# Attention and a gated FFN on one core: weights' parts kept in the buffers from pass to pass, the pairs of chunks taken in the opposite order, and the second pass's sums tied on VectorE

## The chip, the core and the metric

The kernel runs on one core of a Trainium2 chip. Its engines are TensorE (PE: matmuls, and PEld: its weight loads), VectorE (DVE), ScalarE (ACT), GpSimd (POOL) and SyncE (SP), which here issues the DMAs. Each engine takes its instructions in order and waits for the others by semaphores. The metric is the device time of one launch in microseconds (us); less is better.

## The reference

```python
# 8 batches, 8 heads, 576 tokens, head size 64; keys and values averaged over 8 tokens
k_p, v_p = k.reshape(B, H, 72, 8, D).mean(3), v.reshape(B, H, 72, 8, D).mean(3)
attn = softmax(q @ k_p.T / sqrt(D))            # 1e-9 added to the sum
x = (attn @ v_p) -> (B * S, H * D)              # 4608 x 512
out = (sigmoid(x @ w_gate) * (x @ w_val)) @ w_out   # 512 -> 1536 -> 512
```

All is f32. The weights come as 64-bit floats and are converted on the core.

## The kernel before

**Number format.** Each f32 operand is split into a high and a low half that TensorE multiplies at its faster f32 rate (`split`: the high half is a cast on ACT, L103, the low half a subtract on DVE, L104). A product of two operands is three matmuls: high by high, high by low, low by high.

**Passes.** The 4608 tokens are 12 blocks of 384 (`BT`), two blocks (side 0 and side 1) in a pass, six passes, n = 0 to 5. Each pass has a hidden stage (gate G and value V, 12 chunks `f` of 128 hidden columns, or `NP` = 6 pairs `p` of chunks), then the second product with w_out. The attention of the next blocks runs in between: `next(tasks)` lets one piece of it into the program.

- Pass 0 is plain: `hidden_first` converts w_gate and w_val pair by pair, keeps the halves in DRAM (`kept`, and the words themselves in `kept_w`) and multiplies with `whole` (L582). `second` converts w_out chunk by chunk (`convert_o`: the load of `raw_o` L251, the conversion L122 to L132 on ACT and DVE, its halves `oparts`, the stores to `keptO` L258 and `keptwO` L260) and accumulates over all chunks (L717) with `hs`, the halves of the hidden values (L709, L710).
- Passes 1 to 5 take a pair of chunks and the two sides together as 2 by 2 blocks and multiply them with seven products in place of eight (`product`, L542: m = 1 to 7, in the order of `SLOTS`). For that sums of the weights' blocks are needed (`add_up` and `sums`, on DVE) and sums of the operand x (`sums_of_x`, `operands`; their halves are `xo1` to `xo7`, m by m, and plain chunks use `xo1`, `xo2` for side 0 and `xo5`, `xo4` for side 1). `second_sums` does the same for w_out (L808), with reloaded `oparts` (L279, L281) and `hs` of sums (`operand`, L771, L772).
- Pass 1 is mixed: `hidden_second` takes the last two pairs (f = 8 to 11) plain, while the sums for the first four pairs are made, then calls `hidden` for those four.

**Buffers.** `wpool`, "parts", has 8 buffers, just one pair's groups: G and V, each A to D (A, B, C hold two products' parts, 512 KB; D one, 256 KB, in passes 1 to 5). When the last product of a group is issued, `loaded` reloads its buffer for the next pair (L242), and at the end of a pass for pair 0. `big` has 4 buffers that hold `raw_o`, `hs`, the copies `o` of the results, the words `w8` of the weights being summed, and `s1`; `opool` has 4.

**What sets the order.** Nearly everything is put in order by a scheduler that simulates the program as written; it deals the instructions onto the engines, and the buffers of a pool onto its tiles. Only instructions given to `keep_in_program_order` (through `pinned`, or `in_turn` where `tied[0]` is set) stay in the order of the code among themselves. In the kernel before, `tied[0]` is never set. SP issues the loads and the stores in one queue, so an issue that waits holds back the ones behind it.

## Time and profile before

| | |
|---|---|
| runs shown | 998.54, 996.95 and 1000.31 us, median 998.54 |
| profiled execution | 994.61 us, its span 992.8 |
| granted clock of TensorE | 0.991 over the span |
| 0 to 176 us | first blocks' attention, pass 0 hidden |
| 176 to 241.4 us | pass 0, `second` |
| 241.6 to 276 us | pass 1, plain chunks (f = 8 to 11) |
| then to 350, and 350 to 408 us | pass 1: seven products, second product |
| 408, 550, 712 and 868 us | starts of the hidden stages of passes 2, 3, 4 and 5; their second products start at 500, 655, 808 and 950 |

How to read it: the stages are found in the timeline of TensorE, by its lines (L717, L582, L542, L808). The number that counts is TensorE's idle time in a stage and what ended it. A row of waits reads: engine, line that waited, what it waited for, us in total, times, the longest. A row of a timeline reads: start, duration, engine, line, operation, out<-in, count, and in brackets the idle time before and its releaser; "SPq" is SP's queue, where each row is the issuing of DMAs.

### The profile page before, as it was taken

What the parts mean: (1) busy time and instruction counts of PE and PEld (TensorE: products, weight loads), DVE (VectorE), ACT (ScalarE), POOL (GpSimd) and SP (SyncE); (2) the same over time, 40 slices, a digit from 0 to 9 for tenths busy, and PEclk for the clock granted to TensorE, in tenths of its full rate; (3) what the DMA queues carried; (4) which work ended last, traced back from release to release, by engine and by line L of the source; (5) the groups of instructions that cost most, each with busy time, mean ns of one, the idle gap of its engine ahead of it and who ended that gap; (6) DMA issues with size and microseconds to landing.
All of it is one profiled execution on the core that took longest, in us unless ns stands there. A gap on an engine that the chain in (4) does not pass through costs nothing.

```text
span 992.8 us, 15583 instructions
## 1 busy us (share of the span) xinstructions
PE 952.2 (96%) x5436; PEld 914.6 (92%) x5436; DVE 711.3 (72%) x1240; ACT 547.0 (55%) x1113; POOL 49.0 (5%) x67
## 2 busy tenths in 40 slices
PE   5779999989999999999999999999999999999998
PEld 4669999768999999998999999999999999999998
DVE  5767898688798889685588657679366669244474
ACT  4647677545376766564565556556365546233342
POOL 2010000000000100000000000000000100000000
PEclk9989999999999999999999999999999999999999
DMA  9736999876999978899778877787876677877567
GB/s 333 252 118 211 337 367 371 281 262 239 349 332 359 305 239 274 305 391 365 246 254 251 276 240 253 264 283 244 294 260 213 220 256 252 290 229 250 180 198 226
DMA packets 121773, 269.72 MB, mean 272 GB/s; under 512 B 12640, under 2 KB 50272, under 8 KB 120160
## 3 DMA queue, kind: packets, MB, share of 16 engines
q1 hardware_dynamic: 121696, 268.74, 80.2%
q8 instruction: 43, 0.70, 0.3%
q14 instruction: 34, 0.28, 0.1%
HBM read 212.06 MB, written 56.62 MB: 271 GB/s over the span
## 4 chain that ended last, share of the span: by engine, by line
PE 81%; DMA 8%; DVE 7%; ACT 3%; issue 1%; SPq 0%; ACTq 0%; DVEq 0%
PE chain L542 36%; PE acc L808 19%; PE chain L582 12%; PE acc L717 4%; PE sc L368 3%; PE av L377 3%; DMA oparts<-keptS 1%; PE tp L456 1%; PE vp L1011 1%; DVE s L741 1%; DVE hs L772 1%; DMA parts<-keptG1D 1%; DMA keptS<-sums 1%; DMA oparts<-keptO 1%; DMA w<-keptwO 1%
## 5 line engine op out<-in xcount | busy, mean ns | idle before, releaser
L542 PE MATMUL chain<-xo,parts 128*128 128x384 f32 x2352 | 438.3, 340 | 4.1 <-ACT sV L548 2.4
L542 PEld LDWEIGHTS chain<-xo,parts 128*128 128x128 f32 x2352 | 407.6, 188 | 8.2 <-ACT sV L548 3.2
L808 PE MATMUL acc<-hs,oparts 128*128 128x384 f32 x1260 | 229.5, 336 | 5.0 <-DMA oparts<-keptS 2.3
L808 PEld LDWEIGHTS acc<-hs,oparts 128*128 128x128 f32 x1260 | 218.2, 188 | 8.2 <-DVE hs L772 3.5
L582 PE MATMUL chain<-xo,parts 128*128 128x384 f32 x624 | 118.0, 343 | 3.2 <-ACT parts L170 3.1
L582 PEld LDWEIGHTS chain<-xo,parts 128*128 128x128 f32 x624 | 110.1, 191 | 4.9 <-ACT parts L170 3.7
L554 DVE TENSOR_TENSOR y<-chain,sG 128x384 f32<-128x384 f32 x84 | 46.1, 552 | 78.6 <-ACT sG L548 27.2
L554 DVE TENSOR_TENSOR y<-chain,sV 128x384 f32<-128x384 f32 x84 | 45.8, 549 | 43.0 <-PE chain L542 25.4
L450 POOL TENSOR_TENSOR pm<-e,rz 128x384 f32<-128x384 f32 x40 | 37.8, 945 | 682.3 <-DVE rz L431 365.2
L772 DVE TENSOR_TENSOR hs<-h,hs 128x768 fp32r<-128x768 f32 x60 | 57.4, 960 | 15.6 <-ACT hs L771 15.6
L560 ACT ACTIVATE gate<-y 128x384 f32<-128x384 f32 x84 | 43.8, 525 | 41.8 <-DVE y L554 41.4
L771 ACT CAST hs<-h 128x768 fp32r<-128x768 f32 x60 | 50.1, 835 | 30.2 <-PE acc L808 27.5
L548 ACT COPY sG<-chain 128x384 f32<-128x384 f32 x84 | 39.8, 476 | 48.3 <-PE chain L542 47.5
L548 ACT COPY sV<-chain 128x384 f32<-128x384 f32 x84 | 39.9, 476 | 43.1 <-PE chain L542 40.6
L717 PE MATMUL acc<-oparts,hs 128*128 128x512 f32 x216 | 55.1, 407 | 4.1 <-ACT hs L709 4.1
L717 PEld LDWEIGHTS acc<-oparts,hs 128*128 128x128 f32 x216 | 40.6, 193 | 14.1 <-ACT hs L709 5.3
L771 ACT CAST hs<-s 128x768 fp32r<-128x768 f32 x45 | 37.1, 835 | 25.3 <-PE acc L808 17.0
L563 DVE TENSOR_TENSOR h<-y,gate 128x384 f32<-128x384 f32 x84 | 47.5, 568 | 1.9
L772 DVE TENSOR_TENSOR hs<-s,hs 128x768 fp32r<-128x768 f32 x45 | 42.3, 951 | 5.6 <-ACT hs L771 5.3
L368 PE MATMUL sc<-kbd,raw 128*128 128x144 f32 (+1 forms) x256 | 43.2, 298 | 0.4 <-DVE y L554 0.4
L368 PEld LDWEIGHTS sc<-kbd,raw 128*128 128x128 f32 (+1 forms) x256 | 33.9, 177 | 7.9 <-issue 4.7
L460 DVE TENSOR_TENSOR pl<-tp,ph 128x384 fp32r<-128x384 f32 x40 | 22.0, 551 | 17.2 <-ACT ph L459 17.0
(168 smaller groups left out, 1183.5 us busy)
## 6 DMA issues: line engine op xcount, KB each, us to landing
oparts<-keptS SPq DMA_DIRECT2D x60, 512.0 KB, 4.9
oparts<-keptO SPq DMA_DIRECT2D x90, 256.0 KB, 3.8
raw<-in_wgv SPq DMA_DIRECT2D x12, 1024.0 KB, 7.5
raw<-in_qT SPq DMA_DIRECT2D x42, 192.0 KB, 4.7
raw<-in_kT SPq DMA_DIRECT2D x28, 288.0 KB, 5.2
out<-o SPq DMA_DIRECT2D x40, 192.0 KB, 4.7
raw<-in_vm SPq DMA_DIRECT2D x24, 256.0 KB, 4.6
raw_o<-in_wo SPq DMA_DIRECT2D x12, 512.0 KB, 5.9
```

The lines of the kernel that those rows point to most:

```text
L368: nc.tensor.matmul(sc[lo - i * P:hi - i * P, i], lhsT=q[:, lo:hi], rhs=kbd[slot(b, p)], start=True, stop=True)
L450: nc.gpsimd.tensor_tensor(out=pm, in0=e[:, n, :, :KM], in1=rz[:, n, :, None].broadcast_to([P, 2 * QT, KM]), op=ALU.mult)
L542: nc.tensor.matmul(t, lhsT=w[:, h, a], rhs=x[:, y, c], start=(m in (1, 2, 5) and c == 0 and k == 0), stop=(c == 1 and k == 2), skip_group_ ...
L548: nc.scalar.copy(s, t)
L554: nc.vector.tensor_tensor(out=y, in0=t, in1=seen[kind, {2: 1, 3: 6, 7: 5}[m]], op=ALU.add)
L560: nc.scalar.activation(gates[q[0]][:, q[1]], y, AF.Sigmoid)
L563: nc.vector.tensor_tensor(out=hb[f // 4][:, f % 4, q[0] * BT:(q[0] + 1) * BT], in0=y, in1=gates[q[0]][:, q[1]], op=ALU.mult)
L582: nc.tensor.matmul(t, lhsT=w[:, c // 2, h, a], rhs=x[:, y, c % 2], start=(c == 0 and k == 0), stop=(c == NC - 1 and k == 2),)
L717: nc.tensor.matmul(acc[i], lhsT=hs[:, y, a], rhs=o[:, w], start=(f == 0 and k == 0), stop=(f == NF - 1 and k == 2),)
L771: nc.scalar.copy(hs[:, 0], x)
L772: nc.vector.tensor_tensor(out=hs[:, 1], in0=x, in1=hs[:, 0].bitcast(F32), op=ALU.subtract)
L808: nc.tensor.matmul(acc[name, c], lhsT=w[:, k, h, c * P:(c + 1) * P], rhs=hs[:, y, k], start=(m in (1, 2, 5) and i % 3 == 0 and k == 0 and ...
```

## The change

1. `TURNS` gives the order of pairs in each pass: 0 to 3 in pass 1, then 3, 2, 1, 0, 4, 5, then 5 down to 0, 0 up to 5, 5 down to 0. The last pair of a pass is the first of the next, so its parts stay in the buffers (`stays`), and `loaded` no longer reloads at the end of a pass.
2. `reload_plain` goes: the plain chunks f = 8 to 11, made in pass 0, stay in their buffers until pass 1 (`gated` keeps them), and no longer come back from DRAM. Pair 0's parts are now reloaded two groups at a time between those chunks, and the last at their end.
3. In `hidden_second`, `tied[0]` is set around `prepare` and `sums`, so that their first subtracts and the splits of `sums` keep the code's order on ACT and DVE.
4. The thirds of w_out (`qs`) follow the order of the pairs.

```diff
     def sums(kind, p):
...
-        nc.vector.tensor_tensor(out=s[:, 0:2], in0=w[:, 1:3], in1=w[:, 0:2], op=ALU.subtract)
+        in_turn(nc.vector.tensor_tensor(out=s[:, 0:2], in0=w[:, 1:3], in1=w[:, 0:2], op=ALU.subtract))
...
-    def product(kind, p, m):
+    def product(kind, p, m, stays=False):
-        t, w, x = bank[kind, b], parts.pop((kind, p, m)), xo[m]
+        t, w, x = bank[kind, b], parts[kind, p, m] if stays else parts.pop((kind, p, m)), xo[m]
...
     def gated(f, side):
-        if side:
+        if side and f < 2 * EARLY:
             del plain["G", f], plain["V", f]
...
     def hidden_first(tasks):
-        for kind in "GV":
-            for f in range(2):
-                reload_plain(kind, 2 * EARLY + f)
...
+    TURNS = {1: (0, 1, 2, 3), 2: (3, 2, 1, 0, 4, 5), 3: (5, 4, 3, 2, 1, 0), 4: (0, 1, 2, 3, 4, 5), 5: (5, 4, 3, 2, 1, 0)}
...
     def hidden_second(tasks):
+        ring = [("G", "A"), ("G", "B"), ("G", "C"), ("V", "A"), ("G", "D"), ("V", "B"), ("V", "C"), ("V", "D")]
         for i, f in enumerate(range(2 * EARLY, NF)):
-            if f + 2 < NF:
-                for kind in "GV":
-                    reload_plain(kind, f + 2)
             if i < 3:
+                tied[0] = True
                 prepare("GV"[i % 2], i // 2)
+                tied[0] = False
             if i in (2,3,):
+                tied[0] = True
                 sums("O", made_o.pop(0))
+                tied[0] = False
...
+            if i:
+                for _ in range(2):
+                    reload(ring[0][0], 0, ring.pop(0)[1], True)
...
     def hidden(last, tasks, n):
-        pairs = EARLY if n == 1 else NP
-        for p in range(pairs):
+        pairs = TURNS[n]
+        for p, pair in enumerate(pairs):
...
-                product(kind, at, m)
-                loaded(kind, at, m, left, last, pairs, n == 1)
+                stays = at + 1 == len(pairs) and not last
+                product(kind, pairs[at], m, stays)
+                if at + 1 < len(pairs):
+                    loaded(kind, pairs[at], m, left, pairs[at + 1], n == 1)
...
     def second_sums(n, last, build, later):
-                    product("V", pairs - 1, 4)
-                    loaded("V", pairs - 1, 4, {}, last, pairs)
+                    product("V", TURNS[n][-1], 4, not last)
```

The lines of the new program stand 1 to 7 above or below those of the old one (L542 is L535, L582 is L575, L242 is L235, L251 is L244, L260 is L253). The engines' work is the same in number; on SP's queue 48 loads fewer stand. Up to the end of `hidden_first` TensorE's order is the same; behind it the scheduler deals nearly all anew. Three places:

**SP's queue at the end of pass n = 4.** Reloads of parts, and the first loads of w_out's sums (`keptS`) for `second_sums`. Before:

```order
L242 DMA parts<-keptG0C 128x1024
L242 DMA parts<-keptV0A 128x1024
L242 DMA parts<-keptG0D 128x512
L242 DMA parts<-keptV0B 128x1024
L242 DMA parts<-keptV0C 128x1024
L281 DMA oparts<-keptS_208 128x1024
L281 DMA oparts<-keptS_209 128x1024
L242 DMA parts<-keptV0D 128x512
L281 DMA oparts<-keptS_210 128x1024
L281 DMA oparts<-keptS_211 128x1024
L281 DMA oparts<-keptS_212 128x1024
```

After:

```order
L235 DMA parts<-keptV5A 128x1024
L235 DMA parts<-keptG5D 128x512
L235 DMA parts<-keptV5B 128x1024
L235 DMA parts<-keptV5C 128x1024
L235 DMA parts<-keptV5D 128x512
L274 DMA oparts<-keptS_208 128x1024
L274 DMA oparts<-keptS_209 128x1024
L274 DMA oparts<-keptS_210 128x1024
L274 DMA oparts<-keptS_211 128x1024
L274 DMA oparts<-keptS_212 128x1024
```

The reload of V0D, which waits for the last product of the pass, stood among the loads of `keptS`; now the pass's own last part, V5D, is loaded ahead of them, and nothing stands between.

**SP's queue in `second`, from about chunk f = 4 on.** `raw_o` with its buffer's number is one chunk of w_out: before, 2080, 2114, 2148 and 2182 are f = 4 to 7; after, 2068, 2102, 2136, 2170 and 2204 are f = 4 to 8. Before:

```order
L251 DMA raw_o_2148<-in_wo 128x1024
L260 DMA keptwO2_182<-raw_o_2080 128x256 x2
L298 DMA raw_2831<-in_vm 128x512
L258 DMA keptO4_196<-oparts_2087 128x1024
L294 DMA raw_2961<-in_qT 128x384
L251 DMA raw_o_2182<-in_wo 128x1024
L260 DMA keptwO2_182<-raw_o_2114 128x256 x2
L291 DMA raw_2964<-in_kT 128x576
L294 DMA raw_3010<-in_qT 128x384
L258 DMA keptO5_197<-oparts_2121 128x1024
```

After:

```order
L253 DMA keptwO2_182<-raw_o_2068 128x256 x2
L244 DMA raw_o_2102<-in_wo 128x1024
L291 DMA raw_2827<-in_vm 128x512
L251 DMA keptO4_196<-oparts_2075 128x1024
L244 DMA raw_o_2136<-in_wo 128x1024
L287 DMA raw_2937<-in_qT 128x384
L253 DMA keptwO2_182<-raw_o_2102 128x256 x2
L251 DMA keptO5_197<-oparts_2109 128x1024
L244 DMA raw_o_2170<-in_wo 128x1024
L253 DMA keptwO3_185<-raw_o_2136 128x256 x2
L251 DMA keptO6_198<-oparts_2143 128x1024
L244 DMA raw_o_2204<-in_wo 128x1024
```

Before, the load of f = 6 (2148) stands ahead of the store of f = 4's words (keptwO2, from 2080). After, it stands behind it, as those of f = 7 and 8 stand behind the stores of f = 5 and 6; and the load of f = 5 (2102) is behind the store of f = 4. In the new dealing the `raw_o` of f = 4, 6, 8 and 10 have one and the same of the four buffers, those of f = 5, 7, 9 and 11 another.

**DVE and TensorE where the plain chunks of pass 1 begin.** `xo4` is the operand for the second half of side 1, `s4` and `sums` are w_out's sums, `w8` the words of G and V being summed (2589 is G's pair 1, 2890 is V's pair 1). DVE before:

```order
L205 TENSOR_TENSOR s4_2610<-w4_2608 128x512
L415 TENSOR_REDUCE m_2974<-sc_2969 128x6
L206 TENSOR_TENSOR s4_2610<-w4_2608,s4_2610 128x256
L104 TENSOR_TENSOR sums_2614<-s4_2610,sums_2614 128x2x256
L207 TENSOR_TENSOR s4_2610<-w4_2608,s4_2610 128x256
L497 TENSOR_TENSOR s_2463<-xs1_1541 128x768
L694 COPY o_2406<-acc_2026 128x512
L104 TENSOR_TENSOR xo4_2361<-xs1_1541,xo4_2361 128x768
L497 TENSOR_TENSOR s_2464<-s_2463,xs0_966 128x768
L104 TENSOR_TENSOR sums_2619<-s4_2610,sums_2619 128x2x256
L694 COPY o_2413<-acc_2038 128x512
L104 TENSOR_TENSOR xo6_2536<-s_2464,xo6_2536 128x768
```

DVE after:

```order
L190 TENSOR_TENSOR w8_2589<-w8_2589 128x256
L205 TENSOR_TENSOR s4_2596<-w4_2594 128x512
L206 TENSOR_TENSOR s4_2596<-w4_2594,s4_2596 128x256
L207 TENSOR_TENSOR s4_2596<-w4_2594,s4_2596 128x256
L104 TENSOR_TENSOR sums_2600<-s4_2596,sums_2600 128x2x256
L188 TENSOR_TENSOR w8_2890<-w8_2890 128x512
L104 TENSOR_TENSOR sums_2605<-s4_2596,sums_2605 128x2x256
L189 TENSOR_TENSOR w8_2890<-w8_2890 128x256
L490 TENSOR_TENSOR s_2445<-xs1_1541 128x768
L190 TENSOR_TENSOR w8_2890<-w8_2890 128x256
L408 TENSOR_REDUCE m_2576<-sc_2571 128x6
L104 TENSOR_TENSOR xo4_2349<-xs1_1541,xo4_2349 128x768
```

TensorE before, from the last of `second` on (`xo1` and `xo2` are side 0's operands):

```order
L437 MATMUL tp_2697<-identr_89,r3_2693 96x128 x3
L582 MATMUL chain_2435<-xo1_2250,parts_1968 128x384 x6
L582 MATMUL chain_2435<-xo2_2287,parts_1968 128x384 x6
L582 MATMUL chain_2467<-xo5_2324,parts_1968 128x384
L582 MATMUL chain_2449<-xo1_2250,parts_1974 128x384 x6
L582 MATMUL chain_2449<-xo2_2287,parts_1974 128x384 x6
L582 MATMUL chain_2467<-xo5_2324,parts_1968 128x384 x5
L582 MATMUL chain_2467<-xo4_2361,parts_1968 128x384 x6
L582 MATMUL chain_2481<-xo5_2324,parts_1974 128x384 x6
L582 MATMUL chain_2481<-xo4_2361,parts_1974 128x384 x6
```

TensorE after, some 70 matmuls into the plain chunks:

```order
L575 MATMUL chain_2548<-xo5_2312,parts_x_1307 128x384 x3
L370 MATMUL av_1846<-ph_1832,vh1_97 128x384
L370 MATMUL av_1846<-pl_1833,vh1_97 128x384
L370 MATMUL av_1846<-ph_1832,vl1_102 128x384
L370 MATMUL av_1846<-pr_1760,vres1_107 128x384
L575 MATMUL chain_2548<-xo5_2312,parts_x_1307 128x384 x3
L361 MATMUL sc_2571<-kbd4_95,raw_2563 128x144
L361 MATMUL sc_2571<-kbd4_95,raw_2563 64x144
L361 MATMUL sc_2571<-kbd3_94,raw_2563 64x144
L361 MATMUL sc_2571<-kbd3_94,raw_2563 128x144
L575 MATMUL chain_2449<-xo4_2349,parts_1238 128x384
L575 MATMUL chain_2463<-xo4_2349,parts_x_1302 128x384
```

The low half of `xo4` moved on DVE from right behind the first copy of `o` to behind the sums of V's pair 1; on TensorE its first use moved from behind 30 plain matmuls to behind 72, two value products of the attention and a group of scores.

More of the change, by code (lines that the diff above doesn't have):

```diff
@@ L682, in hidden, with loaded @@
             pass
-    def loaded(kind, p, m, left, last, pairs=NP, fresh=False):
+    def loaded(kind, p, m, left, then, fresh):
         g, i = place(m)
         left[kind, p, g] = left.get((kind, p, g), 0) + 1
-        if left[kind, p, g] == sum(m != 8 for m in GROUPS[g]) and not (last and p + 1 == NP):
-            reload(kind, (p + 1) % pairs, g, fresh and p + 1 < pairs)
+        if left[kind, p, g] == sum(m != 8 for m in GROUPS[g]):
+            reload(kind, then, g, fresh)
     def store(o, r, acc, eng):
@@ L755, in third_sums @@
         minus(quarter(q, 1, 0), quarter(q, 0, 0), quarter(q, 1, 0))
-    qs = [(2, 0, 1) if n == 1 else (0, 1, 2) for n in range(NB // 2)]
+    qs = {n: [p // 2 for p in t[::2]] for n, t in TURNS.items()}
+    qs[1] = [2] + qs[1]
     halves = {}
```

20 lines of the change are left out of this document (7 added, 13 removed).

## The prediction

> **What bounds the kernel now.** I read the page first: its busy times, the chain and the queue.
>
> ```profile
> span 992.8 us, 15583 instructions
> PE 952.2 (96%) x5436; PEld 914.6 (92%) x5436; DVE 711.3 (72%) x1240; ACT 547.0 (55%) x1113; POOL 49.0 (5%) x67
> PE 81%; DMA 8%; DVE 7%; ACT 3%; issue 1%; SPq 0%; ACTq 0%; DVEq 0%
> q1 hardware_dynamic: 121696, 268.74, 80.2%
> ```
>
> TensorE is the bound: busy for 96% of the span, and 81% of the chain. The transfers are many, but the chain spends 8% on them. So a change that only takes transfers away can win no more than what TensorE waits for. What it waits for stands in its waits, asked first for the first pass's second product (176 to 242 us), then for all behind it (four of nine rows):
>
> ```profile
> PE acc L717 <- ACT hs L709: 4.1, 3, 2.0
> ...
> PE chain L542 <- ACT sV L548: 2.4, 2, 1.5
> PE acc L808 <- DMA oparts<-keptS: 2.3, 2, 1.6
> PE acc L808 <- DVE hs L772: 2.3, 3, 1.0
> ...
> PE chain L542 <- DMA parts<-keptG1B: 0.4, 1, 0.4
> ```
>
> After 242 us no wait is dear, and reloaded parts are waited for once, for 0.4 us. The table by stage says where there is slack (span, PE, PEld, DVE, ACT, POOL busy, clock, DMA share, GB/s):
>
> ```profile
> 176.00:242.00 66.00, 61.88 (x284) 49.07 (x283) 51.71 (x95) 34.63 (x74) 3.80 (x4) 0.97 0.74 250
> 242.00:266.00 24.00, 24.00 (x139) 24.00 (x138) 22.09 (x41) 11.98 (x23) 0.00 (x0) 1.00 1.02 354
> 266.00:350.00 84.00, 82.02 (x495) 79.70 (x494) 71.75 (x153) 55.92 (x125) 6.87 (x6) 1.00 0.96 329
> ```
>
> From 242 to 266 us, where the second pass's plain chunks run, three resources are full at once: TensorE, DVE (22.09 of 24.00) and the transfers (share 1.02). A different order costs most there.
>
> **The removed transfers.** By the order, 32 reloads at four pass boundaries and 16 reloads of plain chunks go, about 19 of 269.7 MB. The wait above prices them: −0.4 us at most. They are hidden by TensorE's own work, which has the next pair's parts in time. Term −0.4, bounds −0.4 and 0. What goes with them is small: a pass's last pair stays in its eight buffers, its products read it a second time at the start of the next pass, and only then is the second pair of that pass loaded into them, group by group, as between any two pairs before. So the cover of those loads is one pair's products, as it was, and I see no new wait at a pass's start. The buffers of the plain chunks f=8 to 11 that now stay from pass 0 to pass 1 cost no instruction either; their place is the reloads'.
>
> The Trainium skill, "Perfetto Trace Analysis", section "Identifying the Most-Contended Engine", says to work on the engine that is used most, and to judge TensorE by its weight-load share: here 92%, so it is TensorE, as the chain says. By that rule alone 19 MB less on the queues would change nothing, and the sum would be 0.
>
> **The ends of the passes.** SP's queue and TensorE at the end of pass n=4:
>
> ```profile
> 812.04 1.50 SPq L281 DMA_DIRECT2D oparts<-keptS  x2
> 816.03 0.32 SPq L242 DMA_DIRECT2D parts<-keptV0D  x1
> 816.44 4.25 SPq L281 DMA_DIRECT2D oparts<-keptS  x3
> ...
> 815.84 4.85 PE L808 MATMUL acc<-hs,oparts 128*128 128x384 f32 x27
> 822.33 18.99 PE L808 MATMUL acc<-hs,oparts 128*128 128x384 f32 x108 [1.64 <-DMA oparts<-keptS]
> ```
>
> The reload of V0D waits for the last V4 product (the matmuls behind it start at 815.84), and three loads of w_out's sums wait behind it on the queue; TensorE runs dry for 1.64 us. In the new order V5D's load comes earlier, the wrapped reloads are gone, and S_208 to S_212 stand together. So the 1.64 goes. Next late is then an hs from DVE, as at the same point of pass n=3, where the wait is DVE's:
>
> ```profile
> 670.56 4.09 PE L808 MATMUL acc<-hs,oparts 128*128 128x384 f32 x22 [0.86 <-DVE hs L772]
> ```
>
> Of the 2.3 us for oparts the other 0.7 falls in another pass, behind loads that also shared the queue with wrapped reloads; I take half of it. Term −2.0; bounds −2.3 (all) and 0 (hs is as late).
>
> **The second product of pass 0.** No line of it is edited, but its instructions are dealt anew. Its loop of `raw_o` buffers:
>
> ```profile
> 209.87 5.99 PE L717 MATMUL acc<-oparts,hs 128*128 128x512 f32 x18 [1.96 <-ACT hs L709]
> ...
> SPq L251 <- PE acc L717: 7.4, 5, 2.7
> ...
> 178.34 0.52 SPq L251 DMA_DIRECT2D raw_o<-in_wo  x1
> 191.59 0.86 SPq L260 DMA_DIRECT2D keptwO<-raw_o  x2
> 215.89 0.33 SPq L251 DMA_DIRECT2D raw_o<-in_wo  x1
> 225.14 0.84 SPq L260 DMA_DIRECT2D keptwO<-raw_o  x2
> ...
> keptwO<-raw_o SPq DMA_DIRECT2D x24, 128.0 KB, 4.2
> ```
>
> Before, a raw_o load waits for the matmuls of four chunks ago (5 times, 7.4 us on the queue). In the new order the `raw_o` of even and odd chunks share one buffer each, so from f=6 on each load stands right behind the keptwO store of the chunk two before, and must wait until that has landed. A turn is then load to store plus landing: 13.3 us for f=4 (178.34 to 191.59) and 9.3 for f=10 (215.89 to 225.14), plus 4.2. I take 14, nearest to f=10, when DVE had least other work (13.5; f=4 gives 17.5). The chains start earlier, since of 16 plain reloads only three loads, pair 0's first, are left in that part of the queue: I estimate f=4's parts ready at 182 (its load at about 171, not 178.34) and f=5's at 192 (its load is behind f=4's store, some 10 us). Then f=10 is ready at 224, f=11 at 234, and the product, 18 matmuls long per chunk (4.3 us), ends at about 238.5, where before it ended at 241.4: −2.9. But the new order puts two value products and two groups of scores of block 3 behind the stage, which TensorE still has to do:
>
> ```profile
> 184.68 0.34 PE L377 MATMUL av<-ph,vh 128*128 128x384 f32 x1
> ...
> 185.38 1.25 PE L368 MATMUL sc<-kbd,raw 128*128 128x144 f32 x8
> 186.37 4.16 PE L717 MATMUL acc<-oparts,hs 128*128 128x512 f32 x17
> ```
>
> That is 0.7 (184.68 to 185.38) and 1.0 (to 186.37), twice: +3.4. Term +0.5. Bounds: −4.1, all three waits of before gone; and +6.5, with turns of 16 us, as f=11 comes three turns behind f=5, so 6 us later (T at 244.5).
>
> **The plain chunks of pass 1.** This term decides. Let T be the end of the product (241.4 before). xo4 holds half of side 1's tokens' operand. Before, DVE makes its low half at 241.89, right behind the first copy of o, and TensorE has it in time (it is full there). In the new order its low half stands behind `add_up` of V1 (w8_2890): the tied sums keep the program's order on DVE, and the scheduler puts V1's subtract ahead. Rows of before:
>
> ```profile
> 241.60 25.45 PE L582 MATMUL chain<-xo,parts 128*128 128x384 f32 x144
> ...
> 248.56 1.21 SPq L187 DMA_DIRECT2D w<-keptwG  x1
> 252.86 0.32 SPq L187 DMA_DIRECT2D w<-keptwV  x1
> ...
> w<-keptwV SPq DMA_DIRECT2D x6, 512.0 KB, 5.5
> ...
> 238.63 0.60 DVE L415 TENSOR_REDUCE m<-sc 128x6 f32<-128x432 f32 x1
> 240.42 0.95 DVE L497 TENSOR_TENSOR s<-xs 128x768 f32<-128x768 f32 x1
> 241.89 0.95 DVE L104 TENSOR_TENSOR xo<-xs,xo 128x768 fp32r<-128x768 f32 x1
> 258.88 0.68 DVE L188 TENSOR_TENSOR w<-w 128x512 f32<-128x512 f32 x1
> 260.29 0.41 DVE L189 TENSOR_TENSOR w<-w 128x256 f32<-128x256 f32 x1
> ```
>
> V1's words were loaded at T+11.4 (252.86): their buffer is that of an o that has to be stored first, and that stays so. Landing at +5.5 is T+16.9. Behind it DVE does seven rows up to xo4's low half: 0.68 and a sums row of the same size 0.68, 0.41 twice, 0.95, 0.60, 0.95, in all 4.7, so T+21.6. TensorE has before its first use of xo4 in the new order 72 plain matmuls at 0.175 (25.45 over 144, less the tail), 12.6 us, the two value products 1.4, a transpose and scores 1.3, and four matmuls that need the high half alone, 0.7: T+16.0. The wait is 5.6 us. Part of it is given back, as DVE, ACT and the queue go on: the 2.0 us that TensorE idles from 266 to 350 us (82.02 of 84.00) I halve. Term +4.6; bounds 0 (V1's load earlier by 5.6) and +6.
>
> The Trainium skill, "DMA: Bandwidth & Descriptors", section "Anatomy of one DMA — SWDGE (gpsimd) path", fits a DMA as 2.0 us plus bytes over 436e3 per us. It is for another queue than SP's; for 512 KB it would give 3.2 us, where this trace has 5.5. By it the wait would be 3.3 us and the term +2.3; the trace's number is used.
>
> **The tie itself** adds no instruction. What is queued behind the tied subtracts is the rest of the sums, then `parts` and `xo` on DVE; for V1 that is the case above. The rest of passes 1 to 5 is dealt anew with the same work: 0, bounds −2 and +2 from the waits of 2.4 and 2.3 above.
>
> **Sum.** −0.4 −2.0 +0.5 +4.6 +0 = +2.7 us. The profiled execution took 994.6 us, 992.8 of it the span, and 3.9 less than the median of the runs shown, 998.54. On that median the sum gives 1001.2 us. About 0.3%, 3.0 us, is what a measurement of this kernel can tell from no change; so the sum lies just inside it.
>
> **Rivals.**
> - The sum as worked out, a new wait of some 5 us against 2 to 3 saved: 40%. With ±3 us around it, a little over half of its chance is within 0.3%.
> - Faster: V1's words land by T+11.3, so xo4 costs nothing, and raw_o keeps up. −4.1 −2.0 −0.4 = −6.5: 992.0 us, 30%. For it: the removed plain reloads leave the queues emptier, and those of 242 to 266 us were full. Against it: the two waits are in the order, and V1's buffer still waits for the stores. It decides when the load is issued before about T+6.
> - Slower: turns of raw_o of 16 us, T at 244.5: +6.5 +4.6 −2.4 = +8.7, 1007.2 us, 16%. For it: f=4's turn was 17.5. Against: f=10's 13.5. From 14.1 us a turn on, the sum passes +3.0.
> - The change does nothing for the time: waits come and go at equal price, the transfers were hidden anyway: −0.4, 998.1 us, 14%. The Trainium skill's rule of the most-used engine ("Perfetto Trace Analysis", "Identifying the Most-Contended Engine") would come out here.
>
> **How the numbers follow.** Faster by over 0.3%: nearly all of the second case, 30%. Within: the last, 14, and a little over half of the first, 22, together 36%. Slower: the rest of the first, 18, and the third, 16: 34%. The range reaches from just below the second case, 991.5, to the third, 1007.0, leaving out half of the slow case and the far end of the fast one. For the likeliest case alone it is 998 to 1004.5.
>
> **What would show it.** Right: a TensorE wait of 4 to 6 us at the first matmul with xo4's low half, released by DVE's xo, about 16 us after the second product's end; DVE waiting on w from keptwV ahead of it; ACT's raw_o waiting for its DMA late in the product; no wait on oparts from keptS at 822 us's place; SP with 48 DMAs less. Wrong: no wait at xo4, or the product ending below 236 or above 242 us; or new waits for parts at the starts of passes 2 to 5, where the order of pairs turns round and pair p's reload is due sooner than I think.

## The result, and the profile after

| | before | after |
|---|---|---|
| median of six runs (us) | 997.32 (995.91 to 1000.31) | 990.66 (988.31 to 991.94) |
| ratio of the times, 95% interval | | 0.9927 [0.9907, 0.9947] |
| profiled execution, its span (us) | 994.61, 992.8 | 990.34, 988.6 |

The changed kernel is faster by 0.7%, 6.7 us. The two profiled executions are only 4.3 us apart, because that of before is 2.7 below its median. So one profile against one profile cannot account for all of the gain, and single terms of 1 or 2 us are near what it cannot show.

From the page of the changed kernel: its span, the engines' busy time, the chain's shares, the DMA queue.

```profile
span 988.6 us, 15480 instructions
...
PE 951.3 (96%) x5436; PEld 916.1 (93%) x5436; DVE 709.9 (72%) x1240; ACT 545.0 (55%) x1111; POOL 48.8 (5%) x67
...
PE 84%; DMA 6%; DVE 6%; ACT 3%; issue 1%; SPq 0%; DVEq 0%; ACTq 0%
...
q1 hardware_dynamic: 114784, 249.86, 75.0%
```

Some 19 MB fewer are moved, TensorE does the same work in less span, and its share of the chain rose from 81% to 84%. Where its time came from, by two stretches, before and then after (span, PE, PEld, DVE, ACT, POOL busy, granted clock, DMA share, GB/s):

```profile
176.00:260.00 84.00, 79.88 (x387) 67.07 (x386) 68.89 (x125) 44.08 (x90) 3.80 (x4) 0.98 0.81 273
260.00:345.00 85.00, 83.02 (x499) 80.87 (x498) 71.73 (x156) 55.11 (x124) 6.87 (x6) 1.00 0.97 333
```

```profile
176.00:260.00 84.00, 81.48 (x402) 70.70 (x401) 63.90 (x116) 43.89 (x85) 3.27 (x3) 0.98 0.75 250
260.00:345.00 85.00, 85.00 (x520) 83.66 (x519) 77.38 (x163) 58.19 (x130) 6.09 (x6) 1.00 0.86 306
```

Between 176 and 345 us TensorE idled 6.1 us before (4.12 and 1.98) and 2.5 after, and by 345 us it had 36 more matmuls behind it (922 against 886). The rest of the page's gain is spent again later: from pass 1's second product to the end the changed kernel takes 644.7 us, before 640.9. Some 2 us of that is attention that moved behind that point (four value matmuls, six of scores and six transposes more); TensorE's waits from there on are 9.2 us where they were 7.7. TensorE's waits after, in 225 to 345 us (one row, where before had two), and from 338 us on:

```profile
PE chain L575 <- DVE xo L104: 2.5, 1, 2.5
```

```profile
PE acc L809 <- DVE hs L773: 2.7, 4, 1.0
PE chain L535 <- ACT sV L541: 1.5, 1, 1.5
PE chain L535 <- ACT sG L541: 1.5, 1, 1.5
PE chain L535 <- DVE y L547: 1.5, 2, 1.1
PE chain L535 <- DMA parts<-keptV0B: 0.7, 1, 0.7
PE chain L535 <- DMA parts<-keptG1B: 0.7, 1, 0.7
PE acc L809 <- issue: 0.3, 1, 0.3
PE chain L535 <- DMA parts<-keptG3B: 0.3, 1, 0.3
```

The three waits of the second product (4.1 us) and the two on `oparts` (2.3 us) are gone; `xo` in its place costs 2.5 us, and reloaded parts are waited for 1.7 us where it was 0.4. The timeline at the new wait, on TensorE, SP and DVE:

```profile
230.83 2.25 PE L575 MATMUL chain<-xo,parts 128*128 128x384 f32 x12
...
246.93 0.34 PE L575 MATMUL chain<-xo,parts_x 128*128 128x384 f32 x1
249.79 1.97 PE L575 MATMUL chain<-xo,parts 128*128 128x384 f32 x5 [2.52 <-DVE xo L104]
```

```profile
240.66 0.39 SPq L187 DMA_DIRECT2D w<-keptwV  x1
```

```profile
245.52 0.69 DVE L188 TENSOR_TENSOR w<-w 128x512 f32<-128x512 f32 x1 [0.57 <-DMA w<-keptwV]
...
248.79 0.94 DVE L104 TENSOR_TENSOR xo<-xs,xo 128x768 fp32r<-128x768 f32 x1
```

The second product ends at T = 230.8. TensorE is ready for xo4's low half at T+16.4; V1's words are loaded at T+9.8, DVE takes them up at T+14.7 and has the low half made at T+18.9.

### The profile page after: what moved, and what is told of

It is laid out like the page before. It is cut to its first block, busy times and chain, and to the rows that moved or that the text cites. A ratio compares the mean times of both kernels' runs of the same rounds, so it can differ in the third digit from the quotient of the medians.

```text
span 988.6 us, 15480 instructions
## 1 busy us (share of the span) xinstructions
PE 951.3 (96%) x5436; PEld 916.1 (93%) x5436; DVE 709.9 (72%) x1240; ACT 545.0 (55%) x1111; POOL 48.8 (5%) x67
## 4 chain that ended last, share of the span: by engine, by line
PE 84%; DMA 6%; DVE 6%; ACT 3%; issue 1%; SPq 0%; DVEq 0%; ACTq 0%
PE chain L535 38%; PE acc L809 19%; PE chain L575 12%; PE acc L717 5%; PE sc L361 4%; PE av L370 3%; DMA out<-o 1%; PE tp L449 1%; PE vp L1010 1%; DVE s L741 1%; DVE hs L773 1%; DMA parts<-keptV2A 1%; DMA parts<-keptG4B 1%; DMA w<-keptwG 1%; DMA parts<-keptG1B 1%
## 5 line engine op out<-in xcount | busy, mean ns | idle before, releaser
L535 PE MATMUL chain<-xo,parts 128*128 128x384 f32 x2352 | 440.0, 340 | 6.4 <-ACT sV L541 1.5
L535 PEld LDWEIGHTS chain<-xo,parts 128*128 128x128 f32 x2352 | 407.7, 188 | 11.4 <-DVE y L547 2.4
L575 PE MATMUL chain<-xo,parts 128*128 128x384 f32 x552 | 109.3, 351 | 4.5 <-DVE xo L104 2.5
L575 PEld LDWEIGHTS chain<-xo,parts 128*128 128x128 f32 x552 | 100.4, 196 | 6.7 <-DVE xo L104 3.0
L541 ACT COPY sG<-chain 128x384 f32<-128x384 f32 x84 | 40.1, 478 | 54.7 <-PE chain L535 54.5
L773 DVE TENSOR_TENSOR hs<-h,hs 128x768 fp32r<-128x768 f32 x60 | 57.4, 961 | 14.8 <-ACT hs L772 14.7
L717 PE MATMUL acc<-oparts,hs 128*128 128x512 f32 x216 | 52.0, 394 | 0.0
L575 PE MATMUL chain<-xo,parts_x 128*128 128x384 f32 x216 | 43.0, 341 | 0.0
```

Source lines behind the costliest of these rows:

```text
L535: nc.tensor.matmul(t, lhsT=w[:, h, a], rhs=x[:, y, c], start=(m in (1, 2, 5) and c == 0 and k == 0), stop=(c == 1 and k == 2), skip_group_ ...
L541: nc.scalar.copy(s, t)
L575: nc.tensor.matmul(t, lhsT=w[:, c // 2, h, a], rhs=x[:, y, c % 2], start=(c == 0 and k == 0), stop=(c == NC - 1 and k == 2),)
L717: nc.tensor.matmul(acc[i], lhsT=hs[:, y, a], rhs=o[:, w], start=(f == 0 and k == 0), stop=(f == NF - 1 and k == 2),)
L773: nc.vector.tensor_tensor(out=hs[:, 1], in0=x, in1=hs[:, 0].bitcast(F32), op=ALU.subtract)
```

## The experiments

Three readings of each profile stand beside the times, in us. **Second** is pass 0's second product, from the start of its first accumulating matmul to the start of its last, and **next** is from there to pass 1's second product (plain chunks and seven products). **Loss** is TensorE's, from 176 to 345 us: its idle time plus its busy time times one minus the granted clock, added up over stretches of 4 us. Shares are of the kernel before, timed on the same chip at the same time (its medians there were 997.0, 996.8, 995.7, 996.7 and 996.7 us for the five groups). Line numbers differ by a few from kernel to kernel.

| run | what it is | ratio [95%] | median | second | next | loss |
|---|---|---|---|---|---|---|
| before | | 1 | 997.3 | 65.1 | 107.0 | 7.5 |
| after | the change | 0.9927 [0.9907, 0.9947] | 990.7 | 54.4 | 109.6 | 3.6 |
| turns_only | turned order alone | 1.0010 [0.9995, 1.0025] | 998.0 | 68.0 | 107.8 | 11.2 |
| plain_only | plain chunks stay, alone | 1.0016 [1.0000, 1.0032] | 998.2 | 54.9 | 115.9 | 10.0 |
| tie_only | tie alone | 0.9960 [0.9943, 0.9978] | 992.4 | 65.4 | 104.0 | 6.4 |
| no_tie | change without tie | 0.9987 [0.9971, 1.0003] | 996.2 | 55.8 | 115.2 | 9.9 |
| plain_tie | change without turned order | 0.9940 [0.9917, 0.9963] | 990.6 | 55.1 | 110.3 | 4.8 |
| turns_tie | change without plain chunks staying | 0.9980 [0.9959, 1.0000] | 994.1 | 67.9 | 103.0 | 8.7 |
| tie_o_copies | other instructions tied | 0.9989 [0.9972, 1.0006] | 995.9 | 55.8 | 116.5 | 9.0 |
| extra_loads | after, 15 loads more from 154 to 191 us | 0.9980 [0.9958, 1.0002] | 994.7 | 60.8 | 109.0 | 6.1 |
| no_words | before, w_out's words not loaded | 0.9997 [0.9979, 1.0014] | 995.9 | 63.8 | 108.5 | 7.2 |
| after_no_words | after, likewise | 0.9915 [0.9894, 0.9936] | 987.5 | 54.5 | 105.9 | 1.6 |
| v1_tied | after, V1's sums tied too | 0.9957 [0.9940, 0.9974] | 991.5 | 56.3 | 105.6 | 3.9 |
| before_const | before, w_out's sums of a constant | 1.0004 [0.9990, 1.0018] | 996.9 | 65.5 | 106.3 | 7.8 |
| no_tie_const | no_tie, likewise | 1.0005 [0.9990, 1.0020] | 996.9 | 55.6 | 117.5 | 9.2 |
| after_const | after, likewise | 0.9962 [0.9946, 0.9978] | 992.0 | 55.5 | 108.3 | 3.6 |
| tie_prepare | tie around `prepare` alone | 0.9983 [0.9963, 1.0002] | 994.8 | 55.0 | 114.6 | 7.7 |
| behind_xo4 | after, no tie, w_out's sums behind xo4 | 0.9949 [0.9929, 0.9968] | 991.6 | 55.4 | 114.3 | 7.7 |
| before_behind | before, w_out's sums behind xo4 | 0.9959 [0.9937, 0.9982] | 992.7 | 66.6 | 105.0 | 8.9 |
| all_behind | after, V1's sums behind xo4 as well | 0.9947 [0.9926, 0.9968] | 991.4 | 54.5 | 106.2 | 1.5 |

Over these twenty rows loss and ratio go together: their correlation is 0.80, and the fitted line gives 0.08% (0.8 us) of time for each us of loss. That says where the time lies; which edit moves it, the single runs tell. Three things can be read down the columns. In the four pairs that differ by the plain chunks alone, "second" is 10 to 14 us shorter where they stay, and "next" 6 to 9 longer. The tie makes "next" shorter in each of five pairs: 107.0 to 104.0, 107.8 to 103.0, 115.9 to 110.3, 115.2 to 109.6, and 117.5 to 108.3 with the constants. And in the same five pairs it makes the whole faster, by 0.40, 0.30, 0.76, 0.60 and 0.43%.

**The parts of the change, one at a time.**

The turned order alone (part 1 and 4 of the change, in the kernel before):

```diff
+    TURNS = {1: (0, 1, 2, 3), 2: (3, 2, 1, 0, 4, 5), ...
-                product(kind, at, m)
-                loaded(kind, at, m, left, last, pairs, n == 1)
+                product(kind, pairs[at], m, stays)
+                if at + 1 < len(pairs):
+                    loaded(kind, pairs[at], m, left, pairs[at + 1], n == 1)
```

> The turned order of pairs alone (parts stay from pass to pass; plain chunks come back from DRAM as before; nothing tied). Theory 1 (the gain is the emptier queue in pass 0's second product, so it hangs on the plain chunks that stay): only the ends of passes gain, about -1 to -2 us against before, no wait on oparts from keptS, and the second product still has three waits on hs (4.1 us) and ends at about 241 us. Rival 2 (the 32 reloads at the pass boundaries were the cost): -4 to -6 us. Rival 3 (the tie makes the gain): within 1 us of before.

1.0010: nothing gained. The plain chunks that stay, alone (part 2, in the kernel before):

```diff
-        if side:
+        if side and f < 2 * EARLY:
             del plain["G", f], plain["V", f]
...
-                    reload_plain(kind, f + 2)
...
+                    reload(ring[0][0], 0, ring.pop(0)[1], True)
```

> The plain chunks stay in their buffers and pair 0's reloads stand between them; pairs in the old order with the 32 reloads at the boundaries; nothing tied. Theory 1: the second product ends near 231 us without a wait, and most of the gain is there: -3 to -6 us against before; part of it is lost to a longer wait for xo4's low half (4 to 7 us in place of 2.5), since without the tie it stands behind one more set of sums on DVE. Rival 2: about 0. Rival 3: about 0, or slower.

1.0016, nothing gained either, though the last matmul of its second product starts at 230.7 us, as in the changed kernel (230.6). The stage behind it took 115.9 us, against 107.0 before and 109.6 in the changed kernel: most of the 10 us won in one stage is lost in the next. Some 3.4 of the 10 us, by the prediction's price, is attention that only moved behind the second product (eight value matmuls and 16 of scores); and TensorE waits 7.5 us in the next stage, where before it waited 2.0. Its waits in 225 to 345 us:

```profile
PE chain L574 <- ACT xo L103: 2.5, 1, 2.5
PE chain L574 <- DVE xo L104: 2.0, 1, 2.0
PE chain L574 <- ACT o L687: 1.6, 1, 1.6
PE tp L429 <- ACT parts L103: 1.4, 1, 1.4
```

The tie alone (part 3, in the kernel before):

```diff
-        nc.vector.tensor_tensor(out=s[:, 0:2], ...
+        in_turn(nc.vector.tensor_tensor(out=s[:, 0:2], ...
...
+                tied[0] = True
                 prepare("GV"[i % 2], i // 2)
+                tied[0] = False
             if i in (2,3,):
+                tied[0] = True
                 sums("O", made_o.pop(0))
+                tied[0] = False
```

> The kernel before with the sums tied, and nothing else. Theory 1 and rival 2: 0 to -1 us, since DVE's wait of 8.1 us for w_out's words held nobody that TensorE waited for; second product as before, with its three waits. Rival 3: -4 to -6 us.

0.9960: more than half of the gain, from the part that the prediction priced at 0. The change without it (the four lines of `tied[0]` taken out of the changed kernel):

```diff
-                tied[0] = True
                 prepare("GV"[i % 2], i // 2)
-                tied[0] = False
             if i in (2,3,):
-                tied[0] = True
                 sums("O", made_o.pop(0))
-                tied[0] = False
```

> The changed kernel without the tie. Theory 1: TensorE's order up to the plain chunks as in the changed kernel, second product ends near 231 us; xo4's low half is later by the sums of w_out's second third (its words are loaded late), so 2 to 4 us are lost: -3 to -5 us against before. Rival 2: as fast as the changed kernel (-6.7). Rival 3 (the tie makes the gain): 0 to -2 us.

0.9987: of 0.73% only 0.13% is left. What the tie does is seen in DVE's queue where the plain chunks of pass 1 begin. In the kernel before (L205 is the first subtract of w_out's sums; xo4 follows the copy, in a row that the prediction shows):

```profile
238.02 0.69 DVE L205 TENSOR_TENSOR s<-w 128x512 f32<-128x512 f32 x1 [3.88 <-DMA w<-keptwO]
...
241.29 0.68 DVE L694 COPY o<-acc 128x512 f32<-128x512 f32 x1
```

With the tie alone (this profile is some 3 us ahead from the first stage on):

```profile
236.14 0.69 DVE L698 COPY o<-acc 128x512 f32<-128x512 f32 x1
236.74 0.95 DVE L104 TENSOR_TENSOR xo<-xs,xo 128x768 fp32r<-128x768 f32 x1
...
252.55 0.68 DVE L205 TENSOR_TENSOR s<-w 128x512 f32<-128x512 f32 x1
```

Untied, w_out's sums go ahead of the copy of `o` and of xo4, and DVE stands 3.88 us before them for their words; tied, they come 16 us behind the copy. In the kernel before, TensorE's waits show little of it (1.9 us in 225 to 345 us, 0.3 with the tie), and 1.0 us of the 3.0 by which the stage gets shorter is attention that the new order moves behind it. In the changed kernel without the tie it reaches TensorE directly. Its DVE, then ACT, then TensorE:

```profile
231.02 0.83 DVE L205 TENSOR_TENSOR s<-w 128x512 f32<-128x512 f32 x1 [4.08 <-PE acc L713]
```

```profile
231.93 0.62 ACT L103 CAST sums<-s 128x512 fp32r<-128x512 f32 x1 [5.44 <-PE acc L713]
...
233.33 1.07 ACT L692 COPY o<-acc 128x512 f32<-128x512 f32 x2
```

```profile
233.97 2.36 PE L575 MATMUL chain<-xo,parts 128*128 128x384 f32 x12 [1.58 <-ACT o L692]
```

ACT has two casts of the sums in its queue ahead of the copies of `o`; the second product's results are copied 1.6 us late, TensorE's first plain matmul needs that accumulator, and waits. In the changed kernel ACT copies `o` at once and TensorE goes on without a gap.

The two other pairs: the tie and the plain chunks that stay, without the turned order; then the tie and the turned order, without the plain chunks that stay (the edits are those above, put together).

> The changed kernel without the turned order of pairs: plain chunks stay, sums tied, but each pass takes the pairs in the old order and reloads pair 0's parts at its end (32 loads more). Theory 4 (formed after the first four runs: the tie keeps w_out's sums behind the copies of the results, and gives most of the gain; the plain chunks that stay then give pass 0's second product its gain; the turned order little): -4 to -6 us against before. Rival 5 (with the tie in place the turned order is what makes the changed kernel faster than the tie alone): -2 to -4, as the tie without plain chunks that stay.

> The turned order and the tie, while plain chunks come back from DRAM as before. Theory 4: as the tie alone, -3.5 to -5.5 us, at most 1 better through the ends of passes. Rival 5: -6 to -7, as the whole change.

0.9940 and 0.9980. So the plain chunks that stay give nothing alone (+0.16%), and with the tie 0.2% more than the tie alone (0.9940 against 0.9960, intervals that overlap). With the turned order they give 0.23% untied (1.0010 to 0.9987, intervals that overlap) and 0.53% tied (0.9980 to 0.9927, intervals apart). The turned order can be read in four pairs of kernels: +0.10, −0.29, +0.20 and −0.13%. It gives nothing that can be measured.

**Which instructions matter.** First, the copies of `o` tied in place of `prepare`, and w_out's sums tied as before:

```diff
-                tied[0] = True
                 prepare("GV"[i % 2], i // 2)
-                tied[0] = False
...
-            nc.vector.tensor_copy(o, acc)
+            tc.keep_in_program_order(nc.vector.tensor_copy(o, acc))
-            nc.scalar.copy(o, acc)
+            tc.keep_in_program_order(nc.scalar.copy(o, acc))
```

> The changed kernel with another tie: the copies of the results (L694, L696 of the changed kernel) and w_out's sums are kept in the order of the code among themselves, the sums of G and V (prepare) are free. Theory 4: that is the part of the tie that counts, -5.5 to -7 us against before, no wait of TensorE on a copy of o, ACT and DVE don't wait on w_out's words ahead of the copies. Rival 6 (the order of prepare's subtracts against w_out's is what counts): -1 to -3 us, as without a tie.

0.9989, a miss. The wait for the copy of `o` is gone as meant, but others are there, two in the plain chunks (`xo`) and the rest in the seven products:

```profile
PE chain L535 <- ACT sG L541: 2.8, 2, 2.1
PE chain L575 <- ACT xo L103: 1.4, 1, 1.4
PE chain L575 <- DVE xo L104: 0.9, 1, 0.9
PE chain L535 <- ACT sV L541: 0.8, 1, 0.8
PE chain L535 <- DVE y L547: 0.5, 1, 0.5
```

So copies in time, with w_out's sums behind them, are not enough for the gain. Next, more loads: the first three reloads of pair 0 sent six times over, in place of the transfers that the change takes out (built on the changed kernel).

```diff
-        if k:
+        for _ in range(1 + again[0] if k else 0):
             nc.sync.dma_start(
...
+                    again[0] = 5 if len(ring) > 5 else 0
                     reload(ring[0][0], 0, ring.pop(0)[1], True)
+                    again[0] = 0
```

> The changed kernel with 15 loads of 256 KB more on SP's queue near 155 us (the first three loads of pair 0's parts done six times each, same data), about as many bytes as the plain reloads that the change removed there. Theory 1 (rest of it): the emptier queue is what lets the second product run without a wait: with the loads back it waits 3 to 6 us for hs, ends near 236 to 241, and the whole is 2 to 4 us slower than the changed kernel. Rival 7 (the dealing alone does it): the second product stays without a wait unless its dealing changes, and the time within 1.5 us of the changed kernel.

0.9980; the last matmul of the second product starts at 236.7 us, and it waits 4.1 us for `hs` again. But the dealing of the instructions changed with it, so emptier queues and another order were not separated here.

**Is it the words' late load?** (Theory 8.) In two pairs w_out's words were not loaded. First they were set to zero by GpSimd, in the kernel before and in the changed one:

```diff
-        nc.sync.dma_start(w, kept_w[kind, p])
+        if kind == "O":
+            nc.gpsimd.memset(w, 0.0)
+        else:
+            nc.sync.dma_start(w, kept_w[kind, p])
```

> The kernel before, but the words of w_out for its sums aren't loaded: GpSimd sets their buffers to zero (left out: the loads, so the sums in w_out's products are wrong; DVE's and ACT's work on them stays, nothing is tied). Theory 8 (the words of w_out come late, DVE's subtracts that wait for them hold DVE and, behind it, ACT, and the pass-1 stage loses by it; the tie moves those subtracts to where they wait less): -3 to -5 us against before, as the tie alone, all of it between the end of pass 0's second product and pass 1's second product. Rival 9 (the tie gains by another way, such as the order of prepare's subtracts or where its splits stand): 0 to -1.5 us.

> The changed kernel with the same left out (the loads of w_out's words for its sums, zeros in their place). Theory 8: the tie has already taken most of this wait (1.5 us are left on DVE), so at most 1.5 us faster than the changed kernel. Rival 9: 2 to 4 us faster than the changed kernel, as the wait and the tie's gain are two things.

0.9997 and 0.9915. GpSimd itself stood 28 us (225 to 345 us) waiting for buffers in the first, with attention's work behind it, so this pair was no clean reading. Then the sums were taken of a constant that is on the chip, with no load and no GpSimd work, in before, no_tie and after:

```diff
-        w = summing.pop((kind, p))
+        if kind == "O":
+            w = cst[:, 0:1, None].broadcast_to([P, 4, HALF])
+        else:
...
+            w = summing.pop((kind, p))
```

> The kernel before; w_out's sums are made of a constant on the chip in place of its words (left out: their loads; the work on DVE and ACT stays). Unlike in the run with zeros from GpSimd, no other engine can be held by it. Theory 8 (w_out's sums, dealt ahead of their data, hold DVE and ACT in pass 1): -2 to -4 us against before, ACT's and DVE's waits at the sums go from 16 and 8 us to under 8 together. Rival 9 (that waiting costs nothing; the tie gains in another way): within 1 us of before.

> The changed kernel without the tie, w_out's sums made of a constant. Theory 8: most of what the tie gave comes back without it, -4 to -6 us against before (untied it was -1.3); what stays is the wait of the first sums for a buffer that the second product still holds. Rival 9: as untied, 0 to -2 us.

> The changed kernel, w_out's sums made of a constant. Theory 8: the tie has left little to gain, -6.5 to -8.5 us against before. Rival 9: the same or slower than the changed kernel.

1.0004, 1.0005 and 0.9962. With no words to wait for, the untied kernels are no faster, and the tied one still is, by 0.4%. So taking the late load away does not bring the gain, and theory 8 falls as it was put. (In no_tie the row above names another wait anyway: DVE's 4.08 us ended with the second product, which held the buffer.) A cost of the load with the order kept was not separated: with nothing to wait for, more of the sums moved ahead. Their first subtracts stand at 232.4, 239.4 and 245.1 us in before_const, where before has one up to then, at 238.0, and its next at 254.3.

**The wait for xo4.** (Theory 10: V1's sums are queued ahead of it.) In the changed kernel `prepare("V", p + 1)` tied as well, which puts V1's sums far behind xo4:

```diff
+                    tied[0] = True
                     prepare("V", p + 1)
+                    tied[0] = False
```

> The changed kernel with the sums of V in the seven products (prepare in hidden, first V's pair 1) tied too. In the order, V1's subtract goes from ahead of xo4's low half on DVE to 50 rows behind it. Theory 10 (the wait of 2.5 us at xo4 comes from V1's words being loaded late): the wait shrinks to under 1 us, T + 16 us as before, and the whole is 1.5 to 3 us faster than the changed kernel if V1's parts are still in time. Rival 11 (xo4's own chain, the value product's copy and cast on ACT, sets it): the wait stays above 1.5 us. If V1's parts come late, a new wait of TensorE in the first seven products of pair 1 takes the gain.

The cause was as said: of TensorE's waits in 225 to 345 us, that for `xo` falls from 2.5 to 0.8 us.

```profile
PE chain L535 <- DVE h L556: 1.6, 1, 1.6
PE chain L575 <- DVE xo L104: 0.8, 1, 0.8
```

The time did not follow: 0.9957, against 0.9927 for the change. 1.6 us for `h` stands in its place.

**Where the sums are queued.** The tie around `prepare` alone (the two lines of `tied[0]` around `sums` taken out):

```diff
             if i in (2,3,):
-                tied[0] = True
                 sums("O", made_o.pop(0))
-                tied[0] = False
```

> The changed kernel with the tie only around prepare (the sums of G's and V's first pairs), w_out's sums free. In the order, DVE's first subtract of w_out's sums stands ahead of prepare again, V0's stays behind xo4. Theory 8: 0 to -3 us against before, TensorE waits on a copy of o as in the untied run. Rival 12 (prepare's tie is the one that counts, as a tie without it gave -1.1): -5 to -7 us.

0.9983, and the waits of the untied kernel are back (`o` 1.6, `xo` 2.0 and 1.4 us). So w_out's sums have to be held. Then no tie at all, but those sums queued behind xo4's low half (theory 13), in the changed kernel and in the one before; and, in the third, V1's sums too, with `prepare` tied:

```diff
-                tied[0] = True
-                sums("O", made_o.pop(0))
-                tied[0] = False
+                with tc.issue_after(low[4]):
+                    sums("O", made_o.pop(0))
```

> The changed kernel without the tie, but DVE's work for the first two of w_out's sums is queued behind xo4's low half (and nothing else is pinned). Theory 13 (formed after the runs with a constant: what the tie gives is the place of w_out's first sums in DVE's and ACT's queues, ahead of the copies of the results and of xo4 when untied; their work and their buffers hold them, not the load of their words): -4 to -7 us against before, TensorE's waits from 225 to 345 us go from 6 to about 3, no wait on a copy of o. Rival 14 (the rest of the dealing makes it, by chance): 0 to -2 us as untied.

> The kernel before with the first two of w_out's sums queued behind xo4's low half on DVE, nothing else changed. Theory 13: -2.5 to -4.5 us against before, as the tie alone; TensorE's wait on sV in the seven products of pass 1 (1.5 us) gone or under 0.5. Rival 14: within 1 us of before.

> The changed kernel with G's and V's first sums tied as in it, the first two of w_out's sums and the sums of V's pair 1 queued behind xo4's low half on DVE. Theory 10 and 13: TensorE's wait at xo4 falls from 2.5 to under 1 us with V1's sums only a little later, and the whole is 0.5 to 2.5 us faster than the changed kernel (-7 to -9 us against before). Rival 14: anything from -2 to -6 us, with new waits in the seven products or later.

0.9949, 0.9959 and 0.9947. Another way of putting w_out's first sums later gives what the tie gives: 0.41% in the kernel before (tie_only 0.40%), 0.51% with the plain chunks that stay. In time theory 13 is borne out; in its waits only in part. TensorE's in behind_xo4, 225 to 345 us:

```profile
PE chain L537 <- DVE h L558: 2.0, 1, 2.0
PE chain L577 <- DVE xo L104: 1.7, 1, 1.7
PE sc L363 <- DVE e L413: 1.0, 1, 1.0
PE chain L537 <- ACT gate L555: 0.5, 1, 0.5
```

The waits for `o` and for the transposes are gone, but 5.2 us of others are there. behind_xo4 and before_behind are the two that fit the line of loss and time worst (7.7 and 8.9 us of loss with ratios of 0.9949 and 0.9959): their single profiles do not show the gain that their twelve runs have (before's own profile, to which they are compared, is 2.7 us below its median). And all_behind, with the least loss of all the complete kernels (1.5 us), is no faster than the change. No version that computes the whole result beat it.

All twenty kernels can be sorted by one thing in their profiles: whether DVE has w_out's first subtract ahead of its first copy of `o`, or behind. In eight it stands ahead (before, turns_only, plain_only, no_tie, tie_prepare, no_words, before_const, no_tie_const), by 3.0 to 8.5 us; their ratios are 0.9983 to 1.0016. In the twelve others it stands behind, and theirs are 0.9915 to 0.9989. Plain chunks, turned order and dealing vary within both groups, so chance in the dealing (rival 14) is a poor account of the split. But tie_o_copies, with 0.9989, is among the twelve: the place of the sums goes with the gain and does not make all of it.

## Why the prediction was wrong

The likeliest case was 1001.2 us, by a sum of +2.7; it came to 990.7, just below the low end of 991.5. The rival "faster" (992.0, 30%) was nearly met, but its mechanism, xo4 costing nothing, was not what happened: V1's words were loaded at T+9.8, not before T+6. The base of the sum was 1.2 us high too: six runs of the kernel before have a median of 997.32.

- **What bounds the kernel** was right: TensorE, by what it waits for.
- **The removed transfers** (−0.4) were hidden, as said: from 715 to 810 us 198 GB/s are moved where it was 236, and TensorE idles 0.28 us there where it idled not at all. Waits for parts grew by 1.3 us, at 614, 640 and 751 us. These lie inside passes, not at their starts.
- **The ends of the passes** (−2.0): the wait on `oparts` is gone, five loads stand together on SP (808.05), and `hs` from DVE is next, at 0.33 and 0.44 us. The mechanism was right, but turns_only, which has it alone, is no faster. It was given back in other waits, which the sum priced at 0 ± 2.
- **The second product** (+0.5) was mis-sized. The turn of `raw_o` was taken as 14 us and measured 9.9 to 13.4, from one load into a buffer to the next (f = 4, 6, 8 and 10 at 173.44, 186.86, 199.45 and 209.36 us, f = 5 and 7 at 183.36 and 194.51). One part of it is that the store lands in 2.6 us and not 4.2, on emptier queues (a DMA share of 0.75 from 176 to 260 us, before 0.81). So T was 230.8, not 238.5: −10.6 in place of −2.9, without any wait in it. With the 3.4 us of attention that moved behind, the term is −7.2, below its low bound of −4.1. That bound took the three waits at their own length; some 1.7 us more was the slower clock behind the longest of them (last section), and the other 1.4 us is not explained.

```profile
keptwO<-raw_o SPq DMA_DIRECT2D x24, 128.0 KB, 2.6
```

- But this is no net gain by itself: plain_only has the same T, and 1.0016. The sum priced one wait in the stage behind, that for xo4's low half; plain_only has four there, on ACT and DVE, 7.5 us in all. These two engines, which feed the next stage, did not move as far as T did.
- **xo4** (+4.6): place, releaser and cause were right, the size was not: T+16.0 was expected for TensorE's arrival and measured as T+16.4, but the low half was ready at T+18.9, not T+21.6, as V1's words were loaded at T+9.8, not T+11.4, and landed by T+14.7. Their load was issued 1.6 us earlier and took 4.9 us where 5.5 was taken. Hence 2.5 us, not 5.6.
- **The tie itself** (0) is the step that failed most. It was priced by the instructions it adds, none, and by what is queued behind the tied ones. What it keeps back was not priced: w_out's sums, which the scheduler had put ahead of the instructions that release TensorE. A row for that was in the profile of before (DVE 3.88 us before L205, ahead of the copy of `o`). The tie was worth 0.40% alone, and 0.60% in the changed kernel (no_tie against after). One sentence ahead of the prediction led there: that `keep_in_program_order` keeps given instructions in order among themselves. In fact it puts each behind the instruction that stands just before it in the program on its engine, given or not, so even a single tied subtract can no longer be taken ahead of that one.

The gain has two parts, then: later sums of w_out on DVE, shown in three ways (tie_only 0.40%, before_behind 0.41%, and no_tie, which loses 0.6% of 0.73) and by time and "next" in five pairs; and the plain chunks that stay, whose gain is clear of noise in one pair alone, with the tie (0.53%).

**Open.** Which instruction behind the sums makes the gain is not settled. tie_o_copies has nearly the queue of the changed kernel (w_out's first sums behind the copies of `o` and ahead of xo4) and gains 0.1%; what differs on DVE up to there is one `add_up` that stands earlier. Each tie or edge makes the scheduler deal anew, so no run moved the sums and nothing else. Two profiles, of behind_xo4 and before_behind, do not show their gain.

## What to carry to other kernels

When a tie or a pin adds no instruction, ask what the scheduler had hoisted ahead of it: work that is ready early, or not even ready, in the in-order queues of the engines that release the bound one. Here a stage that ended 10 us earlier was worth only what its feeders could follow, so price the next stage together with it, and compare times over some ten runs each before a profile is asked which term moved.

## What the runs showed of the hardware

After an idle time of about 2 us TensorE often runs at a lower granted clock for some 3 to 7 us. The rows (granted clock third from the end) of before, after its wait of 1.96 us, then of after, behind its wait of 2.52 us and in the 4 us behind that:

```profile
209.87:215.70 5.83, 5.83 (x19) 4.56 (x20) 5.83 (x14) 2.80 (x5) 1.06 (x1) 0.71 0.72 261
```

```profile
249.79:253.80 4.01, 4.01 (x15) 4.01 (x16) 3.49 (x7) 1.96 (x4) 0.00 (x0) 0.64 0.43 144
253.84:258.00 4.16, 4.16 (x25) 4.16 (x25) 3.50 (x8) 4.12 (x6) 0.00 (x0) 1.00 0.43 157
```

18 matmuls of the second product took 5.99 us there, and 4.3 elsewhere. So a wait of 2.52 us cost 1.4 us more (4.01 × 0.36). In the twenty profiles, from 176 us on, TensorE has 19 idle times of 1.84 to 2.8 us. Behind 13 of them the granted clock was 0.50 to 0.63 over the next 4 us, behind the six others (1.84 to 2.26 us) it was 1.00. Behind all 17 of 1.5 to 1.75 us it was 1.00. The prediction priced waits at their own length and missed that. The Trainium skill, "TensorE: Matmul & The Clock Gate", section "Part 1: The HAM clock gate (the "warmup" mystery)", has the clock halved after an idle window of about 3.4 us, with windows that run freely. These traces show the lower clock after idle times well below that, from 1.85 us on, though not after each, and not after 1.75 us and less.
